# Top-k attention and two MLPs on one core: sums of squares moved from ScalarE to TensorE, and a shorter tail of the p times v product

## The chip, the cores and the metric

The kernel runs on one core of one Trainium2 chip. TensorE (PE in the profile, PEld its weight loads) multiplies matrices, VectorE is DVE, ScalarE is ACT, GpSimd is POOL, and SP (SyncE) issues nearly all DMAs. The metric is device time in microseconds. Three runs of the kernel before took 1377.99 to 1382.39 us, median 1380.79.

## The reference

Attention over 4 batches, 8 heads, 576 positions and head size 64, in which each row of scores keeps its 32 largest; then two MLPs of 512 to 2048 to 512 over the 2304 tokens. Everything is in FP32, and the weights arrive as float64.

```python
scores = scale * np.matmul(q, k.transpose(0, 1, 3, 2))
kth = np.partition(scores, -top_k, axis=-1)[..., -top_k:-top_k + 1]
scores = np.where(scores >= kth, scores, -1000000000.0)
attn = np.exp(scores - np.max(scores, axis=-1, keepdims=True))
attn = attn / (np.sum(attn, axis=-1, keepdims=True) + 1e-09)
x = np.matmul(attn, v)             # heads side by side: 2304 x 512
h = x @ w_in                       # first MLP
g = np.maximum(h, 0.0) + np.log1p(np.exp(-np.abs(h)))
x = g @ w_out
h = x @ w_in2                      # second MLP
out = (h - np.tanh(h)) @ w_out2
```

## The kernel before

Every product runs on TensorE as three FP16 products: each operand is scaled by a power of two and split into a high and a low FP16 half (hi times hi, hi times lo, lo times hi).

**Attention tiles.** The work is cut into 144 tiles. A normal tile has 128 query rows of one head; a "left" tile takes the last 64 rows of two heads at once. So there are 160 sides, a side being one head's share of a tile. For a tile, `front` computes the scores (L554) and ScalarE copies them out (L557, `ssb`). `chain` lets VectorE find the 32 largest: four searches (L566) and three replacements (L569) of about 0.74 us each. ScalarE computes the exponential (L134, L591), `turn` splits it into halves on ScalarE and GpSimd (L596 to L598) and a DMA transposes them (`pT`). `back` then multiplies p by v into the PSUM tile `px`. A column of ones beside v makes column 64 the sum of the row. Per side `back` issues four times L612, L613 and L614 and once L615, all with 128 rows of contraction; L616, the low half of v's last block, with 64 rows (p's high half); and L618, an FP32 product of one row of ones by a constant, which adds the 1e-9 to the sum. VectorE takes the reciprocal of the sum (L629), ScalarE scales the result (L636), and it is split and transposed into the MLP's input.

**MLP steps.** `gemm1` (L680 to L682) makes a 256-wide slice of h for up to 256 tokens; ScalarE applies the function (L134), GpSimd and ScalarE split it (`g`), and `gemm2` (L723 to L725, L731 to L733) adds the slice's share to the output. The loop over tiles emits one step per tile as soon as its inputs exist, and the rest after the last tile. The second MLP's steps start once all weights are converted.

**Weights.** Each of the four matrices comes in 8 groups of 1024 columns (128 partitions). [...] In `weight_split`, `col_norm` (L169) adds the rows' sums over the partitions by an FP32 product with ones, and `pow2_scale` (L176 to L180) makes the power of two of it. The split follows on VectorE (L304), ScalarE (L305) and GpSimd (L312, L316). In the program's text a group's split comes one call after its conversion.

**What sets the order.** The engines run in order, each its own queue. A scheduler makes the queues when the program is built: it goes by priorities (blocks marked `high_priority` go ahead) and by its own estimate of durations, and a buffer pool's tile is waited for when all its buffers are taken. PSUM's pool `tp` has four buffers for h, `px`, and `col_norm`.

Of the kernel before, what the change touches and what calls it, by code (L numbers as in the profile page):

```python
# [8 lines left out]
F32 = mybir.dt.float32  # L9
F32R = mybir.dt.float32r  # L10
BF16 = mybir.dt.bfloat16
F16 = mybir.dt.float16
I32 = mybir.dt.int32
AF = mybir.ActivationFunctionType
# [59 lines left out]
def topk_attention_two_mlps(  # L74
# [23 lines left out]
    NB = 4  # L98
# [62 lines left out]
    def nm(s):  # L161
        uid[0] += 1
        return f"{s}_{uid[0]}"

    def col_norm(cols, n):

        ps = ps_t.tile([P, 512], F32, tag="tp", name=nm("pn"))
        for i in range(n):
            nc.tensor.matmul(ps[:, 0:1], ones.to_broadcast([P, P]), cols[:, i : i + 1],  # L169
                             start=(i == 0), stop=(i == n - 1))  # L170
        return ps[:, 0:1]

    def pow2_scale(ps, s, inv):

        n = sp.tile([P, 1], I32, tag="n0", name=nm("n0"))
        nc.vector.tensor_scalar(n, ps.bitcast(I32), 24, 23,  # L176
                                op0=ALU.logical_shift_right, op1=ALU.logical_shift_left)

        nc.vector.tensor_scalar(s.bitcast(I32), n, -1.0, float(204 << 23), op0=ALU.mult, op1=ALU.add)
        nc.vector.tensor_scalar(inv.bitcast(I32), n, float(50 << 23), None, op0=ALU.add)  # L180
# [85 lines left out]
    def weight_convert(i, g, parts, used):  # L266

        ss = sp.tile([P, len(parts)], F32, tag="ss", bufs=3, name=nm("ss"))
        for u, (st, cols) in enumerate(parts):
            n = st.shape[1]
            low, high = st[:, :, 0], st[:, :, 1]
            w = high.bitcast(F32)
            nc.scalar.activation(w, w, AF.Copy, scale=float(2.0**-112))
            if LAC[i] == "3":

                top = st.rearrange("p f w -> p (f w)").bitcast(mybir.dt.uint8).rearrange("p (f b) -> p f b", b=8)[:, :, 3]  # L280
                nc.scalar.activation(low, top, AF.Identity, scale=1 / 32, bias=shr)
            elif LAC[i] == "1" or (LAC[i] == "2" and g % 2):

                nc.scalar.activation(low, low.bitcast(U32), AF.Copy, scale=float(0.93 * 2.0**-29))
            else:
                nc.vector.tensor_scalar(low, low, 29, None, op0=ALU.logical_shift_right)
            nc.vector.scalar_tensor_tensor(low, high, 3, low, op0=ALU.logical_shift_left, op1=ALU.bitwise_or)
            nc.scalar.activation(wlo[i][:, cols], low.bitcast(F32), AF.Square, accum_out=ss[:, u : u + 1])
        return i, g, parts, used, ss

    def weight_split(i, g, parts, used, ss):
        s = wsc[i][:, g : g + 1]
        pow2_scale(col_norm(ss, ss.shape[1]), s, winv[i][:, g : g + 1])
        for st, cols in parts:
            low, high = st[:, :, 0], st[:, :, 1]
            w, hi, lo = high.bitcast(F32), whi[i][:, cols], wlo[i][:, cols]
# [83 lines left out]
    def second_scales(sy, iy):  # L380


        wi, wo = winv[2], winv[3]
        if not fixed:
            u, v, icw = tiny(), tiny(), tiny()
            gw = tiny(NG)
            t = sp.tile([P, NG], F32, tag="t", name=nm("t"))
            nc.vector.tensor_mul(t, wi, wo)
            nc.vector.tensor_reduce(u, t, axis=AX.X, op=ALU.max)
            nc.vector.tensor_scalar(icw, u, float(2.0**16), None, op0=ALU.mult)  # L390

            nc.vector.tensor_scalar(v.bitcast(I32), u.bitcast(I32), 255 << 23, None, op0=ALU.bitwise_xor)
            nc.vector.tensor_scalar(gw, wo, v, float(2.0**-17), op0=ALU.mult, op1=ALU.mult)
            fixed.extend((icw, gw))
        icw, gw = fixed
        hin = sp.tile([P, NG], F32, tag="hinb", bufs=3, name=nm("hin"))
        gs = sp.tile([P, NG], F32, tag="gsb", bufs=3, name=nm("gs"))
        ic = sp.tile([P, 1], F32, tag="icb", bufs=3, name=nm("ic"))
        nc.gpsimd.tensor_scalar(hin, wi, iy, 1.0, op0=ALU.mult, op1=ALU.mult)
        nc.gpsimd.tensor_scalar(gs, gw, sy, 1.0, op0=ALU.mult, op1=ALU.mult)  # L400
        nc.gpsimd.tensor_scalar(ic, icw, iy, 1.0, op0=ALU.mult, op1=ALU.mult)
        return hin, gs, ic, None

    def chunk_scales(inv_in, m, add, key):

# [13 lines left out]
        nc.vector.tensor_scalar(mx.bitcast(I32), mx.bitcast(I32), 255 << 23, None, op0=ALU.bitwise_xor)  # L419
        nc.vector.tensor_scalar(mx, mx, float(2.0**13), None, op0=ALU.mult)  # L420
        nc.vector.tensor_scalar(gs, wo, mx, None, op0=ALU.mult)
        hg = sp.tile([P, NG], F32, tag="hg" + key, bufs=bufs, name=nm("hg"))
        nc.vector.tensor_mul(hg, hin, gs)
        return hin, gs, ic, hg


    class Visit:
# [174 lines left out]
    def back(st):  # L602
# [6 lines left out]
        for o, h, c0, c1 in sides:  # L609
# [3 lines left out]
                nc.tensor.matmul(o, st.pT[:, t, c0:c1], vl[:, t, 0 : D + 1], start=False, stop=False)  # L613
                nc.tensor.matmul(o, st.pT[:, NB + 1 + t, c0:c1], vh[:, t, 0 : D + 1], start=False, stop=False)  # L614
            nc.tensor.matmul(o, st.pT[:, NB, c0:c1], vh[:, NB, 0 : D + 1], start=False, stop=False)  # L615
            nc.tensor.matmul(o, st.pT[0:SL, NB, c0:c1], vl[0:SL, NB, 0 : D + 1], start=False, stop=False)  # L616

            nc.tensor.matmul(o[:, D : D + 1], ones[0:1].to_broadcast([1, c1 - c0]), (eps2 if st.soft else eps)[0:1], start=False, stop=True)  # L618
        if st is it.sts[0]:
            it.x = ap.tile([P, 2, P], F16, tag="xs", bufs=NXS, name=nm("xs"))  # L620
            if XE:
# [4 lines left out]

        pv = ps[0:rows, 0 : ns * (D + 1)].rearrange("p (j d) -> p j d", j=ns)
        rr = r[0:rows, 0:ns].unsqueeze(2)
        nc.vector.reciprocal(rr, pv[:, :, D : D + 1])  # L629
        if st.kind == "l":  # L630
            nc.gpsimd.tensor_mul(r[0:rows, 0:ns], r[0:rows, 0:ns], fl[vi.b][0:rows].to_broadcast([rows, ns]))
        for i, (o, h, c0, c1) in enumerate(sides):
# [477 lines left out]
```

## Time and profile before

| | |
|---|---|
| median of three runs | 1380.79 us |
| profiled execution | 1381.37 us, its span 1379.6 us |
| TensorE | 1137.5 us busy (82%), mean granted clock 0.93 |
| VectorE | 994.6 us (72%) |
| ScalarE | 951.4 us (69%) |
| GpSimd | 841.0 us (61%) |
| weight conversion ends (last accumulator read of L288) | 388.5 us |
| last L618 of a side | 1219.9 us |

The busy time of a matmul contains its way through the array, which overlaps the next one. For TensorE the distance from start to start is therefore what it costs, and the timeline gives it. A clock of 1.0 stands for 2.4 GHz, 0.5 for 1.2 GHz; other numbers are means over a stretch.

### The profile page before, as it was taken

The page shows a single profiled execution, that of the slowest core. Times are in us where ns is not written, and L with a number is a line of the kernel's source. Part 1 is how long each engine was busy: PE and PEld are TensorE (multiplying, and loading weights), DVE is VectorE, ACT ScalarE, POOL GpSimd, SP SyncE. Part 2 cuts the span into 40 slices and gives each one's busy share as a digit, 9 for nine tenths or more (in the row PEclk, how much of TensorE's full clock was granted, in tenths as well). Part 3 has the DMA queues.
Part 4 walks back from the last instruction along what each step waited for, and adds up shares of the span by engine and source line. Part 5 has one row for each costly group of instructions (what it writes and reads, how often), then busy time and mean ns, then how long its engine had stood idle before and what let it go on. Part 6 is the DMA issues. An engine that isn't in the chain of part 4 may idle for free.

```text
span 1379.6 us, 28066 instructions
## 1 busy us (share of the span) xinstructions
PE 1137.5 (82%) x10098; PEld 882.1 (64%) x10098; DVE 994.6 (72%) x2150; ACT 951.4 (69%) x1786; POOL 841.0 (61%) x1194
## 2 busy tenths in 40 slices
PE   2232437975479999998999999999999899999998
PEld 1131225864358766767667987687767677896875
DVE  5998879979997697865878679759977688611011
ACT  7987988889886787655666767667764667643332
POOL 2679867887874665644666556557764366543342
PEclk9999998985568999989899999999999799999999
DMA  8956786565666458334456335435543254110000
GB/s 263 277 169 176 205 225 165 110 138 132 159 150 167 102 120 153 64 83 95 91 107 129 74 68 94 90 93 119 119 95 75 45 101 92 28 26 1 17 9 16
DMA packets 322524, 153.18 MB, mean 111 GB/s; under 512 B 270160, under 2 KB 302416, under 8 KB 322384
## 3 DMA queue, kind: packets, MB, share of 16 engines
q1 hardware_dynamic: 322384, 151.39, 47.8%
q8 instruction: 79, 1.29, 0.4%
q14 instruction: 61, 0.50, 0.1%
HBM read 73.04 MB, written 15.37 MB: 64 GB/s over the span
## 4 chain that ended last, share of the span: by engine, by line
PE 55%; DMA 11%; POOL 10%; DVE 9%; ACT 8%; issue 7%; SPq 1%; POOLq 0%; ACTq 0%
PE h L680 8%; PE h L681 8%; PE h L682 8%; DMA pT<-hl 4%; PE y L733 4%; PE y L731 4%; PE y L732 4%; PE s L554 3%; PE y L723 3%; PE y L724 3%; PE y L725 3%; DVE m L566 3%; DVE x L569 2%; PE px L618 2%; POOL wlo L316 2%
## 5 line engine op out<-in xcount | busy, mean ns | idle before, releaser
L566 DVE MAX8 m<-x 128x8 f32<-128x576 f32 x432 | 318.9, 749 | 3.5
L702 POOL TENSOR_SCALAR r<-r,gs 128x512 f32<-128x512 f32 (+1 forms) x160 | 109.1, 682 | 200.3 <-ACT g L701 175.6
L597 POOL TENSOR_TENSOR hl<-x,hl 128x512 f16<-128x512 f32 x144 | 170.4, 1183 | 90.6 <-ACT hl L596 76.7
L569 DVE MATCH_REPLACE8 x<-m,x 128x576 f32<-128x576 f32 x288 | 213.2, 741 | 0.0
L554 PE MATMUL s<-kT,qT 128*128 128x288 f16 x512 | 118.8, 324 | 82.6 <-ACT ssb L557 48.4
L705 POOL TENSOR_TENSOR g<-r,g 128x512 f16<-128x512 f32 (+1 forms) x160 | 172.4, 1078 | 9.4
L134 ACT ACTIVATE r<-h,hin 128x512 f32<-128x512 f32 (+1 forms) x160 | 102.1, 639 | 110.1 <-PE h L682 93.9
L680 PE MATMUL h<-y,whi 128*128 128x256 f16 (+1 forms) x640 | 166.0, 269 | 8.5 <-ACT y L751 8.5
L699 DVE SCALAR_TENSOR_TENSOR r<-h,hin,r 128x512 f32<-128x512 f32 (+1 forms) x80 | 55.1, 690 | 159.5 <-ACT r L134 153.1
L680 PE MATMUL h<-x,whi 128*128 128x256 f16 (+1 forms) x640 | 167.7, 270 | 0.7 <-DMA x<-xs 0.7
L682 PE MATMUL h<-x,wlo 128*128 128x256 f16 (+1 forms) x640 | 167.5, 270 | 0.0
L681 PE MATMUL h<-x,whi 128*128 128x256 f16 (+1 forms) x640 | 167.5, 270 | 0.0
L724 PE MATMUL y<-g,whi 128*128 128x256 f16 (+1 forms) x640 | 164.5, 267 | 2.1 <-POOL g L705 2.1
L681 PE MATMUL h<-y,whi 128*128 128x256 f16 (+1 forms) x640 | 166.0, 268 | 0.0
L682 PE MATMUL h<-y,wlo 128*128 128x256 f16 (+1 forms) x640 | 165.5, 268 | 0.0
L723 PE MATMUL y<-g,whi 128*128 128x256 f16 (+1 forms) x640 | 163.9, 268 | 1.0 <-ACT g L701 0.5
L725 PE MATMUL y<-g,wlo 128*128 128x256 f16 (+1 forms) x640 | 164.4, 267 | 0.0
L701 ACT ACTIVATE g<-r,gs 128x512 f16<-128x512 f32 (+1 forms) x160 | 107.6, 674 | 73.6 <-PE y L724 36.5
L566 DVE MAX8 m<-ssb 128x8 f32<-128x576 f32 x144 | 107.9, 749 | 60.3 <-ACT ssb L557 60.0
L612 PE MATMUL px<-vhl,pT 128*128 128x65 f16 (+1 forms) x640 | 97.5, 209 | 63.0 <-DMA pT<-hl 60.7
L680 PEld LDWEIGHTS <-whi 128*128 128x128 f16 x1280 | 128.2, 100 | 21.6
L681 PEld LDWEIGHTS <-whi 128*128 128x128 f16 x1280 | 127.9, 100 | 19.9 <-issue 1.0
(141 smaller groups left out, 3246.6 us busy)
## 6 DMA issues: line engine op xcount, KB each, us to landing
whi<-in_moe_w_in_dram SPq DMA_DIRECT2D x8, 1024.0 KB, 5.6
wlo<-in_moe_w_in_dram SPq DMA_DIRECT2D x6, 1024.0 KB, 7.5
wlo<-in_moe_w_out_dram SPq DMA_DIRECT2D x6, 1024.0 KB, 5.1
vd<-vhl SPq DMA_DIRECT2D x16, 330.0 KB, 3.2
vhl<-vd SPq DMA_DIRECT2D x16, 330.0 KB, 3.5
kd<-kT SPq DMA_DIRECT2D x32, 160.0 KB, 2.0
whi<-in_moe_w_out_dram SPq DMA_DIRECT2D x5, 1024.0 KB, 4.9
kT<-kd SPq DMA_DIRECT2D x32, 160.0 KB, 2.5
```

Source lines behind the costliest of these rows:

```text
L554: nc.tensor.matmul(ps[:, hf, 0:HS], lhs, rhs[:, hf * HS : (hf + 1) * HS], start=(i == 0), stop=(i == len(prods) - 1))
L566: return lambda: nc.vector.max(m[:, 8 * i : 8 * i + 8], src)
L569: return lambda: nc.vector.match_replace(x, m[:, 8 * i : 8 * i + 8], src, NEG)
L597: nc.gpsimd.tensor_sub(hl[:, S + SL : 2 * S], st.p[:, 0 : NB * P], hl[:, 0 : NB * P])
L680: nc.tensor.matmul(o, hi[:, f], xhi, start=(d == 0), stop=False)
L681: nc.tensor.matmul(o, hi[:, f], xlo, start=False, stop=False)
L682: nc.tensor.matmul(o, lo[:, f], xhi, start=False, stop=(d == ND - 1))
L702: nc.gpsimd.tensor_scalar(r, r, gs, 1.0, op0=ALU.mult, op1=ALU.mult)
L705: nc.gpsimd.tensor_sub(glo, r, ghi)
L723: nc.tensor.matmul(o, hi[:, dd], gh, start=first, stop=False)
L724: nc.tensor.matmul(o, hi[:, dd], gl, start=False, stop=False)
L725: nc.tensor.matmul(o, lo[:, dd], gh, start=False, stop=fin)
```

## The change

Three edits, in `weight_convert`, in `back`, and in what the scale functions return:

1. The sum of squares of a weight group isn't made by ScalarE. The upper 16 bits of each merged 32-bit word are read as BF16 (every fourth half of the staging tile). TensorE multiplies each block of 128 columns by itself and adds the eight products in one PSUM tile of the pool `tp`. The diagonal of that tile holds the columns' sums of squares. VectorE multiplies the tile by an identity and adds up each row, and `col_norm` adds over the partitions, now called at the end of the conversion.
2. In `back`, the low half of v's last block is multiplied with all 128 rows of p's last block (the other 64 hold p's low half for the same positions, so a product of two low halves comes in), the FP32 product of 1e-9 is gone, and a ScalarE ACTIVATE adds the constant on its way from PSUM to SBUF. The reciprocal then works in SBUF.
3. A product `hg` that nobody used is no longer computed (6 small VectorE operations).

```diff
+    class Squares:
+        def __init__(self):
+            self.ps = ps_t.tile([P, 512], F32, tag="tp", name=nm("sq"))
+            self.n = 0
+        def add(self, halves, last):
+            n = halves.shape[1]
+            for o in range(0, n, P):
+                h = halves[:, o : min(o + P, n)]
+                w = h.shape[1]
+                nc.tensor.matmul(self.ps[0:w, 0:w], h, h, start=(self.n == 0), stop=(last and o + P >= n))
+                self.n += 1
+        def total(self):
+            ss = sp.tile([P, 1], F32, tag="ss", bufs=3, name=nm("ss"))
+            d = self.ps[:, 0:P]
+            nc.vector.scalar_tensor_tensor(d, d, 1.0, ident, op0=ALU.mult, op1=ALU.mult, accum_out=ss)
+            return col_norm(ss, 1)
...
-            nc.scalar.activation(wlo[i][:, cols], low.bitcast(F32), AF.Square, accum_out=ss[:, u : u + 1])
-        return i, g, parts, used, ss
+            h = st.rearrange("p f w -> p (f w)").bitcast(BF16).rearrange("p (f h) -> p f h", h=4)[:, :, 1]
+            sq_.add(h, u == len(parts) - 1)
+        return i, g, parts, used, sq_.total()
...
-        pow2_scale(col_norm(ss, ss.shape[1]), s, winv[i][:, g : g + 1])
+        pow2_scale(ss, s, winv[i][:, g : g + 1])
...
-            nc.tensor.matmul(o, st.pT[0:SL, NB, c0:c1], vl[0:SL, NB, 0 : D + 1], start=False, stop=False)
-
-            nc.tensor.matmul(o[:, D : D + 1], ones[0:1].to_broadcast([1, c1 - c0]), (eps2 if st.soft else eps)[0:1], start=False, stop=True)
+
+            nc.tensor.matmul(o, st.pT[:, NB, c0:c1], vl[:, NB, 0 : D + 1], start=False, stop=True)
...
-        nc.vector.reciprocal(rr, pv[:, :, D : D + 1])
+        nc.scalar.activation(rr, pv[:, :, D : D + 1], AF.Identity, bias=(eps2 if st.soft else eps)[0:rows])
+        nc.vector.reciprocal(r[0:rows, 0:ns], r[0:rows, 0:ns])
```

The scheduler places the rest anew. The order of TensorE at the 96th of the 160 sides, before (`px` is the side's product, `pT` the transposed p, `h` the MLP's slice):

```order
L614 LDWEIGHTS pT_9658
L614 MATMUL px_9823<-vhl_8954,pT_9658 128x65
L615 LDWEIGHTS pT_9658
L615 MATMUL px_9823<-vhl_8954,pT_9658 128x65
L616 LDWEIGHTS pT_9658
L616 MATMUL px_9823<-vhl_8954,pT_9658 128x65
L618 MATMUL px_9823<-tiny 128x1
L680 LDWEIGHTS whi_89
L680 MATMUL h_9748<-x_2044,whi_89 128x128
```

and the same side now (lines have moved: L645 is the last product of the side, L751 a step's second product, which was L723):

```order
L642 LDWEIGHTS pT_9893
L642 MATMUL px_10058<-vhl_9191,pT_9893 128x65
L643 LDWEIGHTS pT_9893
L643 MATMUL px_10058<-vhl_9191,pT_9893 128x65
L645 LDWEIGHTS pT_9893
L645 MATMUL px_10058<-vhl_9191,pT_9893 128x65
L751 LDWEIGHTS whi_94
L751 MATMUL y_9795<-g_9661,whi_94 128x128
```

The one-row FP32 product is gone and another MLP product follows the side.

The order of ScalarE at the same side, before (L636 scales the side's product into x; `r` beside it is the reciprocal):

```order
L701 ACTIVATE g_9719<-r_9718,gs_9189 128x256
L134 ACTIVATE r_9773<-h_9748,hin_9188 128x256
L128 ACT_TABLE_LOAD
L134 ACTIVATE ssb_9336<-ssb_9336,m_9487 128x576
L134 ACTIVATE ssb_9525<-ssb_9525,m_9648 128x576
L636 ACTIVATE x_1666_9516<-px_9823,r_1699_9839 128x64
L701 ACTIVATE g_9774<-r_9773,gs_9189 128x256
```

and now (L656 is the added ACTIVATE, L664 the former L636, L585 the former L557, L624 the former L596):

```order
L656 ACTIVATE r_1728_10073<-px_10058,tiny 128x1
L624 CAST hl_10052<-x_9723 128x576
L585 COPY ssb_10085<-s_10080 128x576
L134 ACTIVATE x_9884<-ssb_9760,nb_10189,tiny 128x576
L134 ACTIVATE ssb_9926<-ssb_9926,m_10048 128x576
L664 ACTIVATE x_1695_9750<-px_10058,r_1728_10073 128x64
```

The added instruction stands four places ahead of the scaling here; over all tiles it is none to twelve, most often one to four.

The order of ScalarE near the program's start, before (`wlo` from L288 are the squares, `vst` squares of v and q for their scales, `ssb` the first copy of scores):

```order
L288 ACTIVATE wlo_90,ss_231<-wlo_96 128x1024
L288 ACTIVATE wlo_90,ss_248<-whi_95 128x1024
L477 ACTIVATE khl_136<-kraw_97,tiny 128x5x64
L288 ACTIVATE wlo_90,ss_321<-wlo_96 128x1024
L367 ACTIVATE nst_280,qss_279<-qraw_174 128x256
L343 ACTIVATE vst_564,vss_563<-vst_564 128x460
L557 COPY ssb_164<-s_159 128x576
```

and now (L373 was L343, L505 was L477, L397 was L367, L585 was L557):

```order
L373 ACTIVATE vst_225,vss_212<-vst_225 128x464
L505 ACTIVATE khl_139<-kraw_100,tiny 128x5x64
L397 ACTIVATE nst_312,qss_311<-qraw_188 128x256
L373 ACTIVATE vst_650,vss_649<-vst_650 128x460
L585 COPY ssb_178<-s_173 128x576
```

The copy of the scores has moved up by the four squares that stood ahead of it, of which three are in the piece shown.

## Rows read from the trace of the kernel before

**Rows 1.** The page's busy time by engine, and TensorE's line of 40 slices (each 34.5 us; digits are tenths).

```profile
PE 1137.5 (82%) x10098; PEld 882.1 (64%) x10098; DVE 994.6 (72%) x2150; ACT 951.4 (69%) x1786; POOL 841.0 (61%) x1194
...
PE   2232437975479999998999999999999899999998
```

**Rows 2.** Busy time by stage. Columns: stretch and its length in us, then busy us (and count) of PE, PEld, DVE, ACT, POOL, then the granted clock, the DMA share and GB/s.

```profile
0.00:200.00 200.00, 58.21 (x353) 45.40 (x354) 165.79 (x345) 169.07 (x298) 139.26 (x150) 1.00 0.79 221
200.00:300.00 100.00, 80.39 (x721) 66.33 (x720) 84.83 (x193) 86.18 (x160) 82.07 (x101) 0.93 0.60 140
300.00:390.00 90.00, 48.85 (x354) 37.32 (x352) 83.14 (x191) 76.26 (x182) 66.90 (x107) 0.51 0.62 148
390.00:1225.00 835.00, 800.45 (x7408) 620.67 (x7407) 641.88 (x1389) 569.19 (x1071) 497.74 (x766) 0.95 0.47 96
1225.00:1380.00 155.00, 149.60 (x1274) 112.41 (x1271) 18.92 (x35) 50.67 (x80) 55.05 (x70) 0.99 0.03 10
```

**Rows 3.** Who TensorE waited for from 390 to 1225 us: total us, times, the longest.

```profile
PE s L554 <- ACT ssb L557: 12.4, 9, 3.0
```

**Rows 4.** The same for VectorE and ScalarE in that stage.

```profile
DVE r L629 <- PE px L618: 46.0, 27, 6.7
...
ACT r L134 <- PE h L682: 49.9, 31, 6.9
ACT x L636 <- DVE r L629: 38.2, 27, 3.7
```

**Rows 5.** TensorE's timeline at the end of one side, at full clock: start us, duration us, instruction.

```profile
781.11 0.19 PE L614 MATMUL px<-vhl,pT 128*128 128x65 f16 x1
781.14 0.19 PE L615 MATMUL px<-vhl,pT 128*128 128x65 f16 x1
781.27 0.20 PE L616 MATMUL px<-vhl,pT 64*128 64x65 f16 x1
781.40 0.38 PE L618 MATMUL px<-tiny 1*128 1x1 f32 x2
781.71 0.23 PE L680 MATMUL h<-x,whi 128*128 128x128 f16 x1
781.77 0.22 PE L681 MATMUL h<-x,whi 128*128 128x128 f16 x1
```

**Rows 6.** The same for a side that is mixed with products of h (256 columns each).

```profile
744.58 0.27 PE L681 MATMUL h<-x,whi 128*128 128x256 f16 x1
744.69 0.19 PE L615 MATMUL px<-vhl,pT 128*128 128x65 f16 x1
...
745.81 0.27 PE L680 MATMUL h<-x,whi 128*128 128x256 f16 x1
```

**Rows 7.** Busy time of line L615 (once a side) in the TensorE-bound stage: PE and PEld.

```profile
390.00:1225.00 835.00, 23.95 (x119) 12.29 (x119) 0.95 0.47 96
```

**Rows 8.** VectorE's groups of instructions by line and shape: count, busy us, mean ns of one, idle time before them and its releasers.

```profile
L699 DVE SCALAR_TENSOR_TENSOR r<-h,hin,r 128x512 f32<-128x512 f32 x64 | 47.6, 744 | 96.1 <-ACT r L134 89.7 <-POOL xs L647 6.4
L629 DVE RECIPROCAL r<-px 128x1 f32<-128x1 f32 x128 | 20.1, 157 | 37.3 <-PE px L618 37.0
L699 DVE SCALAR_TENSOR_TENSOR r<-h,hin,r 128x256 f32<-128x256 f32 x16 | 7.5, 476 | 63.4 <-ACT r L134 63.4
L629 DVE RECIPROCAL r<-px 64x2 f32<-64x2 f32 x16 | 2.5, 157 | 18.6 <-PE px L618 18.5
```

**Rows 9.** The same for ScalarE.

```profile
L636 ACT ACTIVATE x<-px,r 128x64 f32<-128x64 f32 x128 | 39.4, 308 | 42.2 <-DVE r L629 40.7 <-DVE tiny L180 1.4
L288 ACT ACTIVATE wlo<-whi 128x1024 f16<-128x1024 f32 x13 | 14.9, 1150 | 0.0
L343 ACT ACTIVATION_READ_ACCUMULATOR vst<-vst 128x1 f32 x60 | 11.3, 189 | 0.0
L288 ACT ACTIVATE wlo<-whi 128x256 f16<-128x256 f32 x5 | 2.1, 423 | 0.1
```

**Rows 10.** Busy time of line L288 by stage (squares and accumulator reads).

```profile
0.00:200.00 200.00, 28.31 (x56) 1.00 0.79 221
200.00:300.00 100.00, 4.98 (x8) 0.93 0.60 140
300.00:390.00 90.00, 11.00 (x42) 0.51 0.62 148
```

**Rows 11.** The FP32 weight loads of the norm, of the groups of instructions over the whole span.

```profile
L169 PEld LDWEIGHTS pn<-ss,tiny 128*128 128x128 f32 x106 | 23.6, 296 | 58.8 <-ACT wlo L288 58.3 <-ACT x L636 0.2
```

**Rows 12.** Waits of TensorE and VectorE from 0 to 390 us.

```profile
PE px L612 <- DMA pT<-hl: 54.5, 19, 13.0
PE pn L169 <- ACT wlo L288: 51.1, 19, 8.0
...
DVE r L629 <- PE px L618: 9.5, 12, 1.7
DVE n L176 <- PE pn L169: 6.3, 6, 2.6
```

**Rows 13.** The chain of work that ended last, from 0 to 390 us, by line (shares of the stretch).

```profile
by line: issue 14.8%; DMA pT<-hl 8.2%; POOL wlo L316 7.6%; DVE x L569 5.7%; DVE m L566 5.2%; POOL hl L597 4.8%; DMA wlo<-in_moe_w_out_dram 3.5%; ACT wlo L288 3.0%; POOL hl L598 2.4%; POOL whi L312 2.4%; DMA wlo<-in_moe_w_in_dram 1.9%; POOL 
```

**Rows 14.** ScalarE's timeline near the start: start us, duration us, instruction.

```profile
20.25 1.19 ACT L288 ACTIVATE wlo<-whi 128x1024 f16<-128x1024 f32 x1
...
28.42 0.61 ACT L557 COPY ssb<-s 128x576 f32<-128x576 f32 x1
```

More of the change, by code (lines that the diff above doesn't have):

```diff
@@ L171, in col_norm @@
         return ps[:, 0:1]
+    ident = cp.tile([P, P], BF16, name="ident")
+    nc.gpsimd.memset(ident, 1.0)
+    nc.gpsimd.affine_select(ident, ident, pattern=[[-1, P]], base=0, channel_multiplier=1,
+                            compare_op=ALU.is_equal, fill=0.0)
+    class Squares:
[14 more added lines that the diff above has]
+            return col_norm(ss, 1)
     def pow2_scale(ps, s, inv):
@@ L266, in weight_convert @@
     def weight_convert(i, g, parts, used):
-        ss = sp.tile([P, len(parts)], F32, tag="ss", bufs=3, name=nm("ss"))
+        sq_ = Squares()
         for u, (st, cols) in enumerate(parts):
@@ L401, in second_scales @@
         nc.gpsimd.tensor_scalar(ic, icw, iy, 1.0, op0=ALU.mult, op1=ALU.mult)
-        return hin, gs, ic, None
+        return hin, gs, ic
     def chunk_scales(inv_in, m, add, key):
@@ L421, in chunk_scales @@
         nc.vector.tensor_scalar(gs, wo, mx, None, op0=ALU.mult)
-        hg = sp.tile([P, NG], F32, tag="hg" + key, bufs=bufs, name=nm("hg"))
-        nc.vector.tensor_mul(hg, hin, gs)
-        return hin, gs, ic, hg
+        return hin, gs, ic
     class Visit:
```

## The prediction

> **What bounds the kernel now.** I read the busy shares by slice first, then one table of busy time by stage that I cut at the slices where the pattern changes. The reader is to see two regimes [rows 1, 2]. Up to about 390 us, while the weights are converted, no engine is alone at its limit: VectorE is busy 165.8 + 84.8 + 83.1 = 333.7 us of 390 (86%), ScalarE 331.5 (85%), TensorE 187.5 (48%). From 390 to 1225 us TensorE is busy 800.5 of 835 us (96%), VectorE 641.9 (77%), ScalarE 569.2 (68%). After 1225 us only MLP steps are left, TensorE at 149.6 of 155 us. So I treat 390 to 1225 us as bound by TensorE, in the order in which its instructions stand.
>
> The waits of TensorE in that stage agree: the longest total is 12.4 us, for ScalarE's copy of the scores [rows 3]. In the same stage VectorE waits 46.0 us for TensorE's last matmul of p times v, and ScalarE 49.9 us for its h [rows 4]. The others wait for TensorE there far more than it for them.
>
> **The change part by part: the tail of p times v.** The timeline of TensorE around one side (a head's share of a tile) shows what the reader must see [rows 5]. The matmuls with 128 rows (L614) start 0.03 us apart. The 64-row one (L616) starts 0.13 us after L615, the one-row FP32 matmul (L618, two passes in the records) 0.13 us after that, and the first matmul of h 0.31 us later. From L615 to h that is 781.71 - 781.14 = 0.57 us. Afterwards two 128-row matmuls stand there, 2 x 0.03 = 0.06 us, so 0.51 us is saved. Where the scheduler mixed the side with matmuls of h, each change of rows is paid separately [rows 6]: from L615 at 744.69 to the L680 at 745.81 are 1.12 us for L615, L616 and four h matmuls. Their regular prices are 2 x 0.03 + 4 x 0.11 = 0.50 us, so 0.62 us is saved. Between these I take 0.55 us.
>
> The stage from 390 to 1225 us has 119 of the 160 sides [rows 7]: 119 x 0.55 = 65 us of TensorE's path (61 to 74 with the two measured prices). The other 41 sides lie before 390 us, where TensorE is half idle; nothing is booked for them.
>
> A rule of the Trainium skill speaks against this term. The page "TensorEngine Tiling (Array Packing)", section "Instruction Overhead", says that a matmul costs a fixed 60 cycles or so, and that one with a single column takes as long as one with 60. By it the added matmul of 65 columns would be as dear as each one-column pass, and removing L618 would be worth next to nothing. The trace disagrees: 0.31 us from L618 to the next start, against 0.03 us between 65-column matmuls [rows 5]. By the rule the sum would be about 1368 us, the fourth case below; by the row it is 1321.
>
> Not all 65 us will arrive. TensorE idles 835 - 800.5 = 34.5 us in this stage now [rows 2]. If the stage shrinks to 770 us, VectorE's 642 us are 83% of it instead of 77%, and TensorE will more often come to a product before its operands. I take off 11 us, a third more of the present idle time. Term: -54 us, own bounds -30 (idle time doubled) and -66.
>
> **1e-9 by ScalarE.** 144 new ACTIVATEs of one or two columns from PSUM, one before each reciprocal (L629, 128 + 16 times [rows 8]). The trace has none of that shape. Bounds: 0.19 us, the accumulator read of one column, below, and 0.31 us, the scaled 128x64 read of the same tile (L636), above [rows 9]. I take 0.25, the latter less 64 columns at the slope by which the 1024-column square (1.15 us) is dearer than the 256-column one (0.42) [rows 9]: 0.95 ns each, 0.06 us. At most 119 x 0.25 = 30 us fall into the TensorE-bound stage, where ScalarE's 569 us leave 266 free; booked at nothing, 30 us if that cover is gone. The chain from product to output gains one operation and one change of engine. In ScalarE's order the new instruction stands some places ahead of the x copy, as the second pair of listings in the section on the change shows. While it waits for TensorE, the casts, copies of scores and exponentials behind it wait too, and VectorE and the scores matmuls wait for those. ScalarE already waits 38.2 us in this stage for the reciprocal [rows 4], which itself waited for TensorE, so most of this wait moves rather than adds. The reciprocal keeps its 0.157 us [rows 8] or loses a little, reading SBUF. Nothing booked.
>
> **The sums of squares.** Removed: 53 Square passes with as many accumulator reads, 28.3 + 5.0 + 11.0 = 44.3 us of ScalarE, all before 390 us [rows 10]. With 41 x 0.25 = 10 us of the new additions, ScalarE there falls by 34 us.
>
> Added on TensorE: 32 x 8 = 256 products of 128 columns and as many weight loads, read with a stride of four halves, for which the trace has no row. From below, 0.055 us, the distance of h matmuls of 128 columns at full clock [rows 5]: 14 us. From above the FP32 weight load of 0.296 us [rows 11]: 76 us. Also 21 fewer columns of the norm. I take 0.08, near the lower end since the row is of the same kind of operand: 20 us, beside 202 us idle before 390 us; booked at nothing, 20 if uncovered.
>
> Added on VectorE: 32 diagonal passes, 128x128 from PSUM. The same instruction took 744 ns at 512 columns and 476 at 256 [rows 8], so 476 - 134 = 342 ns at 128. An accumulator read comes on top (0.2 us on ScalarE [rows 9], nothing shown for VectorE): 0.34 to 0.54, taken 0.4, so 13 us on an engine that is 86% busy. Each pass waits for TensorE, and VectorE's searches (L566, L569) are queued behind it. Waits of that kind cost VectorE 9.5 us in 12 cases and 6.3 us in 6 [rows 12].
>
> What is on the path? The chain up to 390 us has the squares (ACT wlo L288) at 3.0%, 11.7 us [rows 13]. At the start ScalarE is busy without a gap and four squares, the first of 1.19 us, stand before the first copy of scores at 28.42 us [rows 14]; the listings show them gone and the copy moved up, worth about 4 x 1.1 = 4 us and no more, since products and diagonals take their place on the way to the scale. TensorE's own wait of 51.1 us for the squares [rows 12] becomes one for VectorE's shift (L287) and the pass; nothing is won there. So between -25 us (the chain's 11.7 and part of the relieved 34) and +15 (the passes in full and some waiting). I take -6: 4 at the start and a little for ScalarE, against a share of the 13.
>
> **The sum.** Against the profiled execution of 1381.4 us (span 1379.6 and 1.8 around it), which lies 0.6 us over the median of the runs: 1381.4 - 54 - 6 = 1321 us.
>
> **The rivals.**
> Everything arrives: the 66 us in full, since the waits in [rows 4] are for TensorE, and some 20 us from the lighter ScalarE before 390 us. 1381 - 66 - 20 = 1295 us. For it: 85% busy ScalarE and squares on the chain. Against: VectorE's 86% in the same stretch.
>
> Another engine takes over: half of the 65 us is lost because VectorE, at 83%, or the ScalarE additions make TensorE wait, or because its granted clock falls: it is 0.95 in the dense stage and 0.51 from 300 to 390 us, where TensorE is busy 48.9 of 90 us [rows 2]. 1381 - 32 = 1349 us. For it: VectorE's waits are short and many. Against: 96% busy TensorE.
>
> The stall isn't the matmuls': what follows L616 and L618 would have waited anyway, so only 3 starts of 0.03 us go, 0.09 - 0.03 (the 128-row one) = 0.06 a side, 7 us, and 6 before. 1381 - 13 = 1368 us. Against: the rows show no idle time and no releaser before L616, L618 or L680, only their distance [rows 5].
>
> Slower: the diagonal passes hold VectorE's queue. TensorE waits 54.5 us in 19 cases, up to 13.0, for the transposed p before 390 us [rows 12], and a pass whose products are queued behind such a wait stalls VectorE for as long. With 32 x 2.0 = 64 us of waits and 13 of work against 54 won it ends at 1381 - 54 + 77 = 1404 us. It decides from (54 + 4 - 13) / 32 = 1.4 us a pass on. The waits of that kind now are 0.8 to 1.05 us long in the mean and in 18 cases only, so this is unlikely.
>
> **How the numbers follow.** Forecast 62% (1305 to 1338), everything arrives 15%, another engine 16%, no stall 3%, slower 4%. About 0.3% (4 us) is what a measurement of this kernel tells from no change. Faster than that: the first four cases less a little for the weaker ones, 0.93; within it 0.03; slower 0.04. The range goes from 1295 to 1350: it takes in the second case's point and the third's and leaves out their far ends and the last two.
>
> **What would show it.** L618 gone, and from the last 128-row matmul of a side to the next start 0.03 to 0.06 us; the stage of dense TensorE work some 54 us shorter with its idle time at 45 us or so; squares 0.06 to 0.1 us apart; diagonal passes near 0.4 us; additions near 0.25; VectorE's wait in front of a pass under 1 us in the mean; the dense stage beginning between 375 and 395 us. Wrong if the dense stage keeps its 835 us, or begins after 410.

## The result and the profile after

The changed kernel takes 1330.63 us, the median of 4 executions (1323.46 to 1331.81), beside 1381.59 us for the kernel before on the same chip: a ratio of 0.9625, 95% interval 0.9586 to 0.9663, or some 51 us less. The profiled execution took 1331.09 us, with a span of 1329.4 us.

Lines below the new class lie 28 to 30 higher than before: L615 is now L643, the 64-row L616 has become the 128-row L645, L629 is L657, L680 to L682 are L708 to L710. New are L192 (products for the sums of squares), L199 (diagonal pass) and L656 (the addition of 1e-9). VectorE's L287, which joins the two words of a weight by a shift to an FP32 number, is now L316; ScalarE's L288, which squared that number and summed the squares over the row, has no successor.

The page's busy time by engine, and TensorE's line of 40 slices, which answer to [rows 1]:

```profile
PE 1071.8 (81%) x9992; PEld 834.9 (63%) x9992; DVE 992.9 (75%) x2208; ACT 935.0 (70%) x1824; POOL 833.9 (63%) x1196
...
PE   3242436894358998999899999999999799999998
```

Every engine has about as much to do as before but TensorE, which is busy 66 us less. The two regimes are still there. Busy time by stage, in the columns of [rows 2], with the end of the dense stage moved to where it lies now:

```profile
0.00:200.00 200.00, 70.33 (x488) 55.31 (x488) 171.85 (x394) 152.35 (x264) 145.21 (x159) 1.00 0.80 226
200.00:300.00 100.00, 77.94 (x720) 64.79 (x720) 87.04 (x194) 79.45 (x148) 70.00 (x92) 0.93 0.53 124
300.00:390.00 90.00, 37.23 (x290) 25.35 (x290) 78.81 (x195) 66.26 (x148) 62.83 (x105) 0.50 0.64 148
390.00:1172.00 782.00, 733.45 (x7189) 574.02 (x7190) 636.28 (x1393) 584.35 (x1183) 499.29 (x769) 0.95 0.50 103
1172.00:1329.40 157.40, 152.80 (x1309) 115.37 (x1306) 18.93 (x35) 52.60 (x84) 56.53 (x73) 0.99 0.03 10
```

Up to 390 us ScalarE is busy 298.1 us instead of 331.5, 33 less, and VectorE 337.7 instead of 333.7. In the dense stage (from 390 us to the last side) TensorE idles 782 - 733.45 = 48.5 us, where it was 34.5 in [rows 2].

A stretch cut at a fixed time doesn't hold the same work in both kernels. So I cut both at a piece of work: the start of L615 (now L643), which each side has once, at the side that 40 others precede, and at the last side. The first of them is called the 40th here and in the expectations; counted from one it is the 41st. From it to the last one there are 119 sides in both. First the kernel before:

```profile
0.00:385.10 385.10, 182.55 (x1391) 145.14 (x1391) 329.15 (x716) 327.35 (x627) 284.80 (x354) 0.87 0.70 184
385.10:1219.30 834.20, 799.65 (x7370) 619.35 (x7368) 646.34 (x1400) 570.45 (x1075) 499.59 (x767) 0.95 0.47 97
```

And the changed one:

```profile
0.00:394.10 394.10, 188.43 (x1531) 147.94 (x1532) 341.40 (x789) 302.15 (x566) 279.89 (x357) 0.86 0.69 180
394.10:1170.50 776.40, 729.02 (x7133) 570.03 (x7131) 632.43 (x1384) 579.11 (x1173) 497.44 (x766) 0.96 0.50 104
```

The dense stage is 57.8 us shorter, and the 40th side comes 9.0 us later. After the last side some 160 us follow in both. So of the 50 us between the two profiled spans 58 are won in the dense stage, 9 are given back ahead of it, and 1 comes after it. This split hangs on the cut: one side earlier the changed kernel is 16.0 us later, one side later 5.8.

The timeline of TensorE at one side that is mixed with products of h, at full clock, answers to [rows 5, 6]:

```profile
725.58 0.19 PE L643 MATMUL px<-vhl,pT 128*128 128x65 f16 x1
725.61 0.28 PE L709 MATMUL h<-x,whi 128*128 128x256 f16 x1
725.72 0.19 PE L645 MATMUL px<-vhl,pT 128*128 128x65 f16 x1
725.75 0.27 PE L710 MATMUL h<-x,wlo 128*128 128x256 f16 x1
725.86 0.27 PE L708 MATMUL h<-x,whi 128*128 128x256 f16 x1
```

L618 is gone, and no step costs more than its own columns: 0.03 us from either px product to the next start, 0.11 from one h product to the next. The waits in the dense stage, for TensorE, ScalarE and VectorE, with the columns of [rows 3, 4]:

```profile
PE s L582 <- ACT ssb L585: 10.9, 8, 3.6
...
ACT r L134 <- PE h L710: 27.9, 17, 5.9
ACT r L656 <- PE px L645: 22.3, 18, 3.2
ACT x L664 <- DVE r L657: 16.6, 23, 2.3
...
DVE m L594 <- ACT ssb L585: 47.3, 25, 10.3
...
DVE r L657 <- ACT r L656: 23.9, 15, 5.4
```

VectorE's 46.0 us for the end of p times v [rows 4] are now 23.9 us for the addition, and the 22.3 us behind that are ScalarE's for the same product. TensorE's longest total is 10.9 us, as it was 12.4 in [rows 3]: no single wait took the place of what was removed, and its 14 us more of idle time are spread over many short ones.

TensorE's waits before 390 us changed much more; they answer to [rows 12]:

```profile
PE sq L192 <- DVE whi L316: 43.7, 9, 12.3
PE px L640 <- DMA pT<-hl: 41.2, 13, 5.8
PE pn L169 <- DVE sq L199: 27.5, 17, 4.6
...
PE sq L192 <- DVE wst L316: 11.2, 2, 5.8
PE sq L192 <- DVE wlo L316: 9.3, 6, 4.8
...
DVE sq L199 <- PE sq L192: 5.5, 6, 2.1
...
DVE n L205 <- PE pn L169: 7.6, 7, 3.2
```

The 51.1 us of waiting for the squares have become 43.7 + 11.2 + 9.3 = 64.2 us for VectorE's shifts and 27.5 us for the diagonal pass, on an engine that is idle half of that time. VectorE's own wait in front of the pass is small, 5.5 us in all.

The new instructions, from the groups of instructions by line (columns as in [rows 8]):

```profile
L199 DVE SCALAR_TENSOR_TENSOR sq<-sq,ident 128x128 f32<-128x128 f32 x32 | 9.2, 287 | 5.7 <-PE sq L192 5.5
L199 DVE DVE_READ_ACCUMULATOR sq<-sq,ident 128x1 f32 x32 | 4.4, 137 | 0.0
...
L656 ACT ACTIVATE r<-px,tiny 128x1 f32<-128x1 f32 (+1 forms) x144 | 36.7, 257 | 34.8 <-PE px L645 34.2
```

A pass is 287 + 137 = 424 ns, and an addition 257 ns. The reciprocal behind it, now from SBUF, takes 149 ns in the mean instead of 157.

### The profile page after: what moved, and what is told of

Same layout as the page of the kernel before. It is cut to its first block, busy times and chain, and to the rows that moved or that the text cites. A ratio compares the mean times of both kernels' runs of the same rounds, so it can differ in the third digit from the quotient of the medians.

```text
span 1329.4 us, 28005 instructions
## 1 busy us (share of the span) xinstructions
PE 1071.8 (81%) x9992; PEld 834.9 (63%) x9992; DVE 992.9 (75%) x2208; ACT 935.0 (70%) x1824; POOL 833.9 (63%) x1196
## 4 chain that ended last, share of the span: by engine, by line
PE 37%; DMA 14%; DVE 13%; ACT 13%; POOL 12%; issue 8%; SPq 2%; POOLq 0%; ACTq 0%; DVEq 0%
PE h L710 5%; PE h L708 5%; PE h L709 5%; DMA pT<-hl 5%; DVE m L594 4%; DVE x L597 4%; POOL hl L625 3%; PE y L760 2%; PE y L759 2%; PE y L761 2%; PE y L751 2%; PE y L752 2%; PE y L753 2%; PE s L582 2%; POOL g L733 2%
## 5 line engine op out<-in xcount | busy, mean ns | idle before, releaser
L625 POOL TENSOR_TENSOR hl<-x,hl 128x512 f16<-128x512 f32 x144 | 173.1, 1202 | 96.2 <-ACT hl L624 86.8
L708 PE MATMUL h<-y,whi 128*128 128x256 f16 (+1 forms) x640 | 164.4, 266 | 9.7 <-ACT y L779 9.3
L708 PE MATMUL h<-x,whi 128*128 128x256 f16 (+1 forms) x640 | 165.6, 268 | 4.1 <-DMA x<-xs 3.6
L751 PE MATMUL y<-g,whi 128*128 128x256 f16 (+1 forms) x640 | 163.6, 266 | 5.3 <-ACT o L791 3.3
L710 PE MATMUL h<-x,wlo 128*128 128x256 f16 (+1 forms) x640 | 165.6, 268 | 0.0
L709 PE MATMUL h<-x,whi 128*128 128x256 f16 (+1 forms) x640 | 165.5, 267 | 0.0
L710 PE MATMUL h<-y,wlo 128*128 128x256 f16 (+1 forms) x640 | 164.1, 266 | 0.0
L709 PE MATMUL h<-y,whi 128*128 128x256 f16 (+1 forms) x640 | 164.1, 265 | 0.0
L708 PEld LDWEIGHTS <-whi 128*128 128x128 f16 x1280 | 127.6, 100 | 20.5 <-issue 0.3
L640 PE MATMUL px<-vhl,pT 128*128 128x65 f16 (+1 forms) x640 | 96.9, 208 | 52.9 <-DMA pT<-hl 51.8
```

The costliest lines, as they stand in the source:

```text
L625: nc.gpsimd.tensor_sub(hl[:, S + SL : 2 * S], st.p[:, 0 : NB * P], hl[:, 0 : NB * P])
L708: nc.tensor.matmul(o, hi[:, f], xhi, start=(d == 0), stop=False)
L709: nc.tensor.matmul(o, hi[:, f], xlo, start=False, stop=False)
L710: nc.tensor.matmul(o, lo[:, f], xhi, start=False, stop=(d == ND - 1))
L751: nc.tensor.matmul(o, hi[:, dd], gh, start=first, stop=False)
```

## The experiments

The theory was that the gain is TensorE's starts at the end of p times v, and that the rest is worth little. The main rival was that the lighter ScalarE ahead of 390 us pays for some of it; another, that parts of the change stand in each other's way. Each ratio below is against the kernel before on the same chip, with its 95% interval. Differences in us are of medians, often from different chips, where the kernel before took 1379 to 1384 us; where the ratios give another figure it stands beside. The listings leave `nc.`, the engine's name before `matmul` and `reciprocal`, and unchanged lines out.

**One half of the change each.** The new end of p times v alone, with the squares left on ScalarE, in the line numbers of before (the product `hg` stays):

```diff
-  matmul(o, st.pT[0:SL, NB, c0:c1], vl[0:SL, NB, 0 : D + 1], start=False, stop=False)
+  matmul(o, st.pT[:, NB, c0:c1], vl[:, NB, 0 : D + 1], start=False, stop=True)
...
-  matmul(o[:, D : D + 1], ones[0:1]..., (eps2 if st.soft else eps)[0:1], start=False, stop=True)
...
-  reciprocal(rr, pv[:, :, D : D + 1])
+  scalar.activation(rr, pv[:, :, D : D + 1], AF.Identity, bias=(eps2 if st.soft else eps)[0:rows])
+  reciprocal(r[0:rows, 0:ns], r[0:rows, 0:ns])
```

> The new tail of p times v alone (128 rows for the last product, the add on ScalarE); the squares stay on ScalarE. If the whole gain is TensorE's starts in the dense stage and the squares are worth nothing: about 1326 us, the last product of a side at 1168 to 1175 us, and the 40th side near 385 us as in the kernel before. If the squares' move cost the 9 us by which the 40th side came later in the changed kernel: 1322 us or below. If the lighter ScalarE carried part of the gain: 1340 us or more.

Measured: 1331.02 us, ratio 0.9645 (0.9615 to 0.9676). And the sums of squares on TensorE alone, with those three edits undone in the changed kernel (the product `hg` is gone here too, and was not measured by itself):

> The sums of squares on TensorE alone; the tail of p times v stays as before. If they are worth nothing: within 5 us of 1381. If the diagonal passes on VectorE and the waits of TensorE for the shifts cost what the 40th side showed: 1388 to 1392 us. If the 34 us less of ScalarE count: 1361 us.

Measured: 1378.36 us, ratio 0.9995 (0.9968 to 1.0023). The end of p times v gives all of the gain, and the move of the squares nothing that can be measured, though it takes 33 us off ScalarE. The dense stage, cut at the sides as above, is 782.7 us long in the first and 823.6 in the second.

**The end of p times v, taken apart.** 128 rows for L616, with L618 left where it was:

```diff
-  matmul(o, st.pT[0:SL, NB, c0:c1], vl[0:SL, NB, 0 : D + 1], start=False, stop=False)
+  matmul(o, st.pT[:, NB, c0:c1], vl[:, NB, 0 : D + 1], start=False, stop=False)
```

> Only the last low-half product gets 128 rows; the one-row FP32 product stays, squares and reciprocal too. If each matmul is charged by its own distance as the timeline of before shows (0.13 us in front of the 64-row one, 0.03 in front of a 128-row one): 0.10 us less a side, 12 us, 1369 us. If a change of rows between neighbours is what costs, and 64 to 1 is as dear as 128 to 1, a whole change goes in mixed sides too: up to 0.2 us a side, 1357 us. If only columns counted: 1381 us.

Measured: 1370.52 us, ratio 0.9947 (0.9926 to 0.9968), 9 us less (7 by the ratio). TensorE's timeline at one side:

```profile
789.59 0.20 PE L615 MATMUL px<-vhl,pT 128*128 128x65 f16 x1
789.63 0.19 PE L616 MATMUL px<-vhl,pT 128*128 128x65 f16 x1
789.75 0.38 PE L618 MATMUL px<-tiny 1*128 1x1 f32 x2
790.06 0.23 PE L680 MATMUL h<-x,whi 128*128 128x128 f16 x1
```

From L615 to L680 it is 0.47 us, against 0.57 in [rows 5]; over 119 sides that is 12 us. The two profiles list the same instructions in the same order on every engine, so this gain isn't the scheduler's. Then the other way round, L618 taken out and 1e-9 added by ScalarE, while L616 keeps its 64 rows:

```diff
-  matmul(o, st.pT[0:SL, NB, c0:c1], vl[0:SL, NB, 0 : D + 1], start=False, stop=False)
+  matmul(o, st.pT[0:SL, NB, c0:c1], vl[0:SL, NB, 0 : D + 1], start=False, stop=True)
...
-  matmul(o[:, D : D + 1], ones[0:1]..., (eps2 if st.soft else eps)[0:1], start=False, stop=True)
...
-  reciprocal(rr, pv[:, :, D : D + 1])
+  scalar.activation(rr, pv[:, :, D : D + 1], AF.Identity, bias=(eps2 if st.soft else eps)[0:rows])
+  reciprocal(r[0:rows, 0:ns], r[0:rows, 0:ns])
```

> Only the 1e-9 moves to ScalarE; the last low-half product keeps its 64 rows, squares stay on ScalarE. By the distances of before, 0.26 to 0.30 us remain of the 0.57 from the last 128-row product to the next start: 119 x 0.29 = 35 us less, 1346 us. If a one-column product is as cheap as a 60-column one, 119 x 0.06 = 7 us: 1374 us. If the added ScalarE instruction holds back its queue: over 1360 us with longer waits of TensorE for the copy of scores.

Measured: 1340.93 us, ratio 0.9727 (0.9688 to 0.9766), 38 us less. Its timeline:

```profile
778.47 0.20 PE L615 MATMUL px<-vhl,pT 128*128 128x65 f16 x1
778.60 0.20 PE L616 MATMUL px<-vhl,pT 64*128 64x65 f16 x1
778.74 0.23 PE L723 MATMUL y<-g,whi 128*128 128x128 f16 x1
```

The 64-row product still costs 0.13 us ahead of it and 0.14 behind, 0.27 us up to the next product; the 0.30 us of L618 are gone, 36 us over 119 sides.

Each edit by itself comes out within 3 us of its distances: 9 for 12, and 38 for 36. Together they don't. By the distances both are worth 0.57 - 0.06 = 0.51 us a side, or 61 us, which is more than 12 + 36, since each edit alone leaves a change of rows standing; measured are 48. Between L618 gone alone and both edits (1340.93 to 1331.02 us) the order is again the same on every engine: by the distances the 128 rows are worth 0.21 us a side there, 25 us, and they bring 10 (11 by the ratios).

Where the rest goes can be reckoned from the traces. TensorE's work at full clock is its busy time in the dense stage less half of what ran at 1.2 GHz (by the trace's record of the granted clock; the contiguous products measured below take 0.107 us at 1.2 GHz against 0.056 at 2.4). All figures are us, from one profile of each kernel:

| kernel | dense stage | TensorE idle | busy at 1.2 GHz | work at full clock |
|---|---|---|---|---|
| before | 834.2 | 34.6 | 82.9 | 758.2 |
| squares on TensorE alone | 823.6 | 29.6 | 74.3 | 756.8 |
| 128 rows alone | 823.7 | 39.0 | 81.9 | 743.7 |
| L618 gone alone | 797.1 | 41.5 | 63.7 | 723.8 |
| both: the new end alone | 782.7 | 52.4 | 52.7 | 703.9 |
| the whole change | 776.3 | 47.4 | 52.9 | 702.4 |

The work falls by 14.5 us for the rows, 34.4 for L618 and 54.3 for both, in the pattern of the distances; with both, idle time rises by 18 us and takes part of it back. In the six further kernels below that have the new end and the old priorities the work is 701 to 703 us, whatever their order; in the two with other priorities it is 695 and 692, and why is open. So the gain comes from TensorE's starts at the end of p times v, and doesn't need a lucky order.

**The addition on ScalarE.** The changed kernel with the reciprocal straight from PSUM and no addition, and the same without the sums on TensorE:

```diff
-  scalar.activation(rr, pv[:, :, D : D + 1], AF.Identity, bias=(eps2 if st.soft else eps)[0:rows])
-  reciprocal(r[0:rows, 0:ns], r[0:rows, 0:ns])
+  reciprocal(rr, pv[:, :, D : D + 1])
```

> The changed kernel without the added ScalarE instruction: VectorE takes the reciprocal from PSUM again, and 1e-9 (a thousandth of the last bit of a sum of 1, or less) is left out. If the add is hidden, as booked: 1331 us within 5. If its stop in ScalarE's queue (it waited 34 us in all for TensorE) is what keeps the dense stage from shrinking by the full 65 us: 1321 us or below, TensorE's idle time in the stage back to about 35 us.

Measured: 1312.30 us, ratio 0.9520 (0.9484 to 0.9557). The time is that of the second case, 1321 us or below, but its sign isn't there: TensorE's idle time in the dense stage is 41.7 us and not 35. (1e-9 is about a hundredth of the last bit of an FP32 sum of 1, not a thousandth.)

> The shorter tail without the added instruction (1e-9 left out), squares on ScalarE as before. If neither the add nor the squares' place counts: 1331 us within 5. If the add counts: 1321 us.

Measured: 1354.92 us, ratio 0.9819 (0.9777 to 0.9861). Here neither case of the expectation came. With the sums on TensorE, leaving the addition out wins 18 us (14 by the ratios); with the squares on ScalarE it loses 24. No price of one instruction has both signs. The second kernel does less work than the one with the new end alone, and is slower: from 390 to 1170 us TensorE waits 25.9 us for the copies of the scores (19.1 of them in its dense stage), where it waited 9.0; it is busy at 1.2 GHz for 70.3 us of its dense stage instead of 52.7, and its 40th side comes at 398.7 us instead of 386.1. TensorE's work at full clock is the same, 702.7 us. What differs besides the instruction is the order in which the scheduler puts everything once it is missing.

**What the order alone is worth.** The changed kernel with two of the scheduler's priorities changed (weight blocks 40 for 100, tiles 60 for 50) and every instruction kept; and the slower kernel of the last pair with the same two numbers:

```diff
-HPW = 100
+HPW = 40
...
-HP = 50
+HP = 60
```

> The changed kernel, the same instructions, with the weights' blocks at priority 40 for 100 and the tiles' at 60 for 50, so that the scheduler makes another order from the first 100 us on. If differences of 10 to 25 us between versions come from the order that the scheduler happens to make: off 1331 us by 8 us or more, most of it before the 40th side. If the order matters little: 1331 us within 5.

Measured: 1311.57 us, ratio 0.9487 (0.9458 to 0.9516).

> The short tail without the add and with the squares on ScalarE (1354.92 us), under the same two other priorities. If its 24 us over the version with the add are the order's: 1340 us or below, with the 40th side before 392 us. If leaving out the add is dearer there by its nature: 1355 us within 5.

Measured: 1331.35 us, ratio 0.9625 (0.9591 to 0.9658). The same instructions in another order are worth 19 us in the one and 24 in the other (27 by the ratios), as much as leaving the addition out. The stages of the first, cut at the same counts of sides (its profiled execution, 1305.40 us, is the shortest of the six):

```profile
0.00:380.40 380.40, 189.38 (x1535) 147.33 (x1536) 338.78 (x795) 303.80 (x569) 283.66 (x363) 0.88 0.71 188
380.40:1144.50 764.10, 715.93 (x7128) 566.61 (x7126) 628.12 (x1378) 576.21 (x1169) 492.62 (x760) 0.97 0.51 105
```

It comes to the 40th side 13.7 us earlier than the changed kernel, and its dense stage is 12.3 us shorter. TensorE's idle time there is the same (764.1 - 715.9 = 48.2 us); its granted clock is 0.97 instead of 0.96, and its work at full clock 695 us instead of 702. So an effect under some 20 us that comes with another order can't be told here. That holds for the addition and for the squares, and not for the 128 rows, which left the order as it was.

**What a product for the sums costs.** In a single execution, each group got 24 further products whose result nobody reads: the strided halves as weights against the contiguous identity matrix, the identity as weights with the strided halves streamed, and both contiguous:

```diff
+  if last:
+      extra = ps_t.tile([P, 512], F32, tag="tp", name=nm("ex"))
+      for j, (a, b) in enumerate(((h, ident), (ident, h), (ident, ident))):
+          for o in range(8):
+              matmul(extra[:, 0:P], a, b, start=(j + o == 0), stop=(j + o == 9))
```

> The changed kernel with 24 more products a group into a PSUM tile that nobody reads: eight with strided weights and contiguous columns, eight with contiguous weights and strided columns, eight with both contiguous. The squares themselves (both strided) started 0.118 us apart at either clock. If the strided read of the streamed columns is what is slow: 0.118 for the second kind, 0.056 for the first and third. If it is the strided weight load: 0.118 for the first kind, 0.056 for the second and third. If BF16 itself or the identity is at fault: 0.118 for the third as well.

TensorE's timeline (the number behind x is how many products a row joins):

```profile
24.26 1.09 PE L198 MATMUL ex<-wlo,ident 128*128 128x128 bf16 x8
25.17 0.63 PE L198 MATMUL ex<-ident 128*128 128x128 bf16 x8
25.63 0.34 PE L169 MATMUL pn<-ss,tiny 128*128 128x1 f32 x2
```

Eight products with strided halves as the stream take (25.17 - 24.26) / 8 = 0.114 us each from start to start, eight contiguous ones (25.63 - 25.17) / 8 = 0.058. Over all groups the medians at full clock are 0.056 us where the weights alone are strided, 0.116 where the stream is, 0.117 with both and 0.056 with neither; at half the clock 0.107, 0.116, 0.118 and 0.107. So the strided weight load shows no price of its own, and the strided stream takes twice as long as a contiguous one at full clock, at a pace that TensorE's clock hardly changes. The 256 products of the change are 256 x 0.118 = 30 us. The execution took 1339.30 us, 9 more than the median of the changed kernel, with 768 products more that by these prices take 58 to 84 us: most of such work ahead of the dense stage is covered, though one execution in one order doesn't say how much.

**The sums left out.** Four constants of the size of the sums stand in for them; products, passes and squares are gone, and the norms stay:

```diff
-  return i, g, parts, used, sq_.total()
+  return i, g, parts, used, col_norm(known[i], 1)
...
```

> The changed kernel with no sum of squares at all: constants close to the sums stand in their place, so the 256 products, the 32 diagonal passes and the squares are left out; the product over the partitions stays. If the work of the sums, wherever it is done, doesn't set the pace before 390 us: 1331 us within 5, the 40th side near 390 us. If the waits of TensorE for the shifts (64 us) or the 13 us of passes do: 1315 to 1322 us with the 40th side at 380 us or before.

Measured: 1298.22 us, ratio 0.9417 (0.9383 to 0.9452), 32 us under the changed kernel (29 by the ratios) and under every case of the expectation. Its longest wait of TensorE up to 390 us:

```profile
PE px L642 <- DMA pT<-hl: 97.1, 26, 10.9
```

The waits for shifts and passes have mostly become waits for the transposed p: other work is late instead. The dense stage stays at 777.4 us, and the 40th side comes at 365.6, earlier than in any kernel here that has sums (379.8 at best). That speaks for a cost of the sums ahead of the dense stage, wherever they are made; since orders differ by some 20 us, the 32 don't say how much of it is theirs. Whether it is their work, their place in the queues or the buffer of `tp` that they hold isn't shown.

**The sums a step later.** If TensorE's 64 us of waiting for shifts were the price, moving products, pass and norm from weight_convert to the head of the next step, when the shifts are long done, should win it back:

```diff
-        sq_ = Squares()
-            sq_.add(h, u == len(parts) - 1)
...
+    def weight_split(i, g, parts, used):
+        sq_ = Squares()
+        ...
+        ss = sq_.total()
```

> The changed kernel with the products, the diagonal pass and the norm of a weight group moved from its conversion to its split, one call later, when the shift that they read is long done. If TensorE's waits for the shifts (64 us before 390 us, ahead of scores and p times v in its queue) are what the sums cost: 1305 to 1320 us, these waits nearly gone and the 40th side at 375 us or before (366 without any sums). If the passes on VectorE or the products' own time are: 1331 us within 6, 40th side near 394. If the later scale delays the splits: over 1337 us.

Measured: 1353.28 us, ratio 0.9789 (0.9756 to 0.9823). TensorE's waits up to 390 us:

```profile
PE sq L192 <- DVE whi L315: 29.1, 6, 10.0
PE pn L169 <- DVE sq L199: 26.2, 16, 6.0
...
PE sq L192 <- DVE wlo L315: 14.5, 5, 6.4
...
PE sq L192 <- DVE wst L315: 3.1, 2, 2.8
```

The waits for shifts shrank from 64.2 us to 29.1 + 14.5 + 3.1 = 46.7, which is not the "nearly gone" that the theory asked for, so it wasn't put to the test. The 40th side came at 414.4 us and the whole took 23 us longer, as in the third case; whether the later scale did it, as that case has it, or the order isn't shown. With the addition left out as well:

> The same without the added ScalarE instruction (1e-9 left out). If the two effects add: 18 us below the kernel with the sums at the split. If the 18 us of leaving out the add came by the order that the scheduler happened to make: anything within 15 us of it.

Measured: 1324.89 us, ratio 0.9583 (0.9555 to 0.9612), 28 us less than with it and 13 (9 by the ratios) more than the changed kernel without the addition: a third size for the same edit, 10 us from the 18 that the first case asked for and within the 15 that the second allowed.

## Why the prediction was right

The forecast was 1321 us (1295 to 1350); 1330.6 lies 10 us above it, on the likeliest case. The dense stage was to win 54 us and won 58; ahead of it 6 us were to be won and 9 were lost.

**The end of p times v** was right in its mechanism, and most of what the distances promise shows in TensorE's work. The term by itself is the fall of TensorE's work at full clock, 758.2 - 702.4 = 55.8 us over 119 sides, 0.47 us a side where I took 0.55: 9 us less than the 65. About a third of the sides of the kernel before (35 of the 106 whose end ran at full clock) are mixed like the one of [rows 6], so 0.55 is a fair mean of the two distances; why the work fell by less is open.

The rule of the Trainium skill that the prediction weighed against this term ("TensorEngine Tiling (Array Packing)", "Instruction Overhead") doesn't hold for these products. By it the two edits would have been worth 7 us together; taking out the one-column product and its FP32 passes was worth 38 us by itself, with the addition that replaced it. That product differs from its neighbours in its rows and its type as well as its columns, and no run takes these apart.

**The new idle time** was put at 11 us and is 47.4 - 34.6 = 12.8 us. Unforeseen was the clock: TensorE was busy at 1.2 GHz for 82.9 us of this stage before and for 52.9 after, worth 15.0. The rival on another engine had named a falling clock. In stretches of 100 us from 400 to 1200 the granted clock was 0.90, 0.97, 0.88, 0.97, 0.97, 1.00, 0.89, 0.99 before and 0.91, 0.97, 0.93, 1.00, 0.94, 0.98, 0.95, 1.00 after. Why the time at 1.2 GHz fell is not shown: the stretches hold different work, and each kernel has one profile. (Over the whole span the four executions of the changed kernel had mean clocks of 0.901 to 0.938, without the time following them.) So the 58 us of the dense stage are 56 + 15 - 13, where the forecast was 65 - 11. That 54 comes so near is in part luck: a term 9 us too large and a clock that nobody had booked.

**1e-9 by ScalarE.** The additions were put at 0.25 us each and booked at nothing; they measured 0.257. What they cost in the whole stays open. In the changed kernel leaving them out wins 18 us, with the sums at the split 28, and with the squares on ScalarE it loses 24. TensorE's work in the dense stage is the same without them.

**The sums of squares.** The diagonal pass was put at 0.4 us (0.424), VectorE's wait for a pass at under 1 us (5.5 us in 6 cases), ScalarE's relief at 34 us (33). A product was put at 0.08 us and took 0.118: a quarter of the way up from the lower bound and not beside it, because the strided halves are streamed as well as loaded as weights. That is 30 us and not 20, on an engine with some 200 idle there. The step that failed is the sum of -6 ahead of the dense stage: the 40th side came 9.0 us later. That it is the squares is indicated by two pairs (386.1 to 394.1 us with the new end of p times v, 385.1 to 392.5 with the old one), but where the addition is left out it is 398.7 to 379.8 the other way. A term of a few us there was more than the profile could give; the bounds of -25 to +15 were the honest part of it. With +9 for -6 this step is 15 us off, more than the 10 us by which the forecast missed.

**The rivals.** "No stall" and "slower" are refuted by the two halves of the end of p times v and by VectorE's waits. "Everything arrives" fell ahead of 390 us: a ScalarE that is 33 us lighter brought nothing, as VectorE (86%) had suggested. "Another engine" has its sign: TensorE idles more, by 13 us where 11 had been allowed for it. (Its 1349 us leave out the 6 us that the forecast and the case of no stall book ahead of the dense stage; with them it is 1343.)

Of the kernels that are faster than the changed one, only the one with the two other priorities leaves nothing out: 1311.6 us, a further 19 us for two numbers.

## What to carry to other kernels

In a stage that one engine bounds, read that engine's timeline from start to start: there a product of one row or of 64 rows among products of 128 showed a price that its busy time doesn't, and the distances, times their count, came out to within 3 us of the gain of either edit alone. The two together brought 48 of the 61 us that the distances promise, while TensorE's idle time rose. Where no engine was at its limit, a lighter ScalarE won nothing here, and a term of a few us was a guess. And where a scheduler sets the order, measure what another order of the same instructions is worth before believing an edit's price; here it was 19 to 24 us, as much as leaving the additions out. An edit that leaves the order as it was, like the 128 rows here, needs no such control.

## What the runs showed of the hardware

- A product of 128 columns with BF16 halves eight bytes apart as its stream takes 0.116 us from start to start, at either clock, against 0.056 contiguous at 2.4 GHz. The same stride on the weights shows no price (0.056 us).
- A change of rows has a price on each side of it: 0.13 us ahead of the 64-row product and 0.14 behind it, where products of 65 columns otherwise start 0.03 us apart. From the one-row FP32 product to the next it is 0.31 us; there rows and type change at once.
- VectorE's reading of the accumulator shows as an instruction of its own, 137 ns behind each pass of 287 ns.
